# Row dots on VectorE in the first chain, turned blocks copied by ScalarE in the second: a decode backward pass on one core

## The chip, the cores and the metric

The kernel runs on one core of a Trainium2 chip. The metric is device time in microseconds (us) of one execution; lower is better. A core has TensorE (PE; its weight loads are listed as PEld), VectorE (DVE), ScalarE (ACT), GpSimd (POOL), SyncE (SP) and 16 DMA engines. Here SyncE issues the loads and GpSimd the stores.

## The reference

A transformer block for one decoded token in a batch of two, forward and backward: adaptive layer norm, attention over a cache of 8192 keys in 32 heads, then a gated MLP. The gradients of both caches are outputs, and they and the caches are nearly all of the traffic. The part that the change touches is the backward pass of the MLP, for each batch element b:

```python
h   = layernorm(x) * (1 + cb) + sb            # called h2 in the kernel, 512 wide
gate, up = h @ w1, h @ w3                     # w1, w3: 512 x 1376
out = (silu(gate) * up) @ w2                  # w2: 1376 x 512
# wanted here:  d_h2 = w3 @ d_up + w1 @ d_gate   (w1, w3 lie in SBUF with their 512 rows on partitions)
```

## The kernel before

The program is laid out in numbered slots; in each slot every engine gets a little work of several jobs. A head is a job of 8 slots. There are 64 heads (32 for each batch element), and each has two jobs: a *first pass* reads K and V (4 MiB); a *second pass* reads V again and writes the gradients of K and V (6 MiB). Between them stand two *chains*, one for each batch element, of small dependent steps: attention output, layer norm, MLP forward and backward. Second passes of an element can start only after its chain. So the order is: first passes alone; the first chain beside first passes; a mixed stage of first and second passes; the second chain beside second passes; second passes alone with the weight gradients; and a tail.

In both chains the gradient of h2 was made by turning: TensorE transposes eight 128x128 blocks of w3 or w1 (four in the last group of each) into PSUM, VectorE copies them to SBUF, TensorE multiplies them by the vector in the next slot. Twelve such groups take 13 slots.

```python
def turned_steps(put, groups, done):
    def tr(k):
        ...                                                     # cut
        for j, src in enumerate(blocks):
            nc.tensor.transpose(tp[:r, j, :], src, identb[:])
        kt = ktp.tile([P, GRP, P], BF16, name="kt", tag="kt")
        nc.vector.tensor_copy(kt[:r, 0:len(blocks), :], tp[:r, 0:len(blocks), :])
        st[("t", k)] = kt
    ...                                                         # cut
    for k in range(len(groups) + 1):
        put(1, lambda k=k: step(k))                             # one slot each
```

The length of the first chain decides how many first passes come before the second passes:

```python
E0 = CS0 + length(ch[0])
TC = E0 + 5
while len(sA) < NHD and s < TC:      # sA: first slots of first passes, sC: of second passes
    sA.append(s); s += NG            # NG = 8 slots
...                                  # then first and second passes in turn
CS1 = end_a(sA[NHD - 1]) + 1         # the second chain follows the last first pass
```

After each chain, `steps_do` turns blocks of the output projection in the same manner, one group of two heads at a time.

## Time and profile before

The median is 1759.24 us over 20 runs (1756.26 to 1765.01). The profile was taken in a run of 1762.17 us. From its page, the span, the busy times and the transfers:

```profile
span 1760.4 us, 55279 instructions
...
PE 1389.0 (79%) x24266; PEld 1243.7 (71%) x24266; DVE 1181.6 (67%) x1697; ACT 953.3 (54%) x1370; POOL 391.9 (22%) x685
...
DMA packets 114847, 713.59 MB, mean 405 GB/s; under 512 B 11392, under 2 KB 20300, under 8 KB 33196
```

| Stretch (us) | what runs | GB/s | DMA share |
|---|---|---|---|
| 40 to 280 | first passes alone | 416 | 1.01 |
| 360 to 500 | first chain and its wake | 388 | 1.00 |
| 500 to 1080 | mixed | 413 | 1.01 |
| 1080 to 1200 | second chain | 381 | 0.99 |
| 1250 to 1680 | second passes, weight gradients | 415 | 1.01 |
| 1690 to 1740 | tail | 393 | 0.97 |

No engine is busy all the time, but the DMA engines nearly are: the kernel is bound by its 713.59 MB. An engine's busy time matters only where it keeps transfers from being issued. There are two such places in the middle. The table by stretch (window; busy us and number of instructions of PE, PEld, DVE, ACT, POOL; granted TensorE clock, 1.00 being full speed; DMA share; GB/s) shows the first one, the first chain's turns and their wake (the shortage of transfers that follows them). DMA share is the mean busy share of the 16 DMA engines, which the view can give as slightly over 1:

```profile
core 0: us, PE busy (x) PEld busy (x) DVE busy (x) ACT busy (x) POOL busy (x), PEclk, DMA share, GB/s
420.00:440.00 20.00, 18.19 (x379) 16.21 (x378) 14.54 (x36) 8.50 (x12) 1.89 (x7) 1.00 1.00 401
440.00:460.00 20.00, 18.95 (x397) 18.01 (x393) 16.35 (x23) 13.41 (x21) 7.22 (x12) 1.00 0.98 373
460.00:480.00 20.00, 18.42 (x382) 16.27 (x383) 12.61 (x16) 13.35 (x19) 4.51 (x11) 1.00 1.00 387
480.00:500.00 20.00, 17.37 (x319) 16.32 (x317) 15.23 (x23) 9.47 (x13) 5.50 (x9) 0.91 1.00 390
```

and the second one, the second chain's turns:

```profile
1130.00:1140.00 10.00, 7.94 (x158) 7.69 (x156) 7.51 (x23) 6.64 (x11) 0.93 (x2) 0.50 0.91 357
1140.00:1150.00 10.00, 8.44 (x163) 8.14 (x161) 9.46 (x25) 4.05 (x4) 1.59 (x3) 0.67 0.91 343
1150.00:1160.00 10.00, 8.18 (x158) 7.68 (x155) 9.57 (x19) 3.57 (x6) 1.06 (x2) 0.83 0.99 350
1160.00:1170.00 10.00, 8.73 (x142) 8.47 (x139) 8.73 (x18) 3.27 (x4) 1.07 (x2) 0.66 0.91 333
```

In the first TensorE is busiest (18.2 of 20 us), in the second VectorE (up to 9.57 of 10). The timeline of VectorE (start, duration, line, operation) shows the pace of the first chain's turns. L689 is the copy of a turned group, one per slot; L885 copies the result of the group before:

```profile
408.32 0.69 DVE L689 COPY kt<-tp 128x1024 bf16<-128x1024 bf16 x1 [1.05 <-PE tp L687]
408.93 0.16 DVE L885 COPY dacc<-s_ps 128x4 f32<-128x4 f32 x1
...
410.52 0.69 DVE L689 COPY kt<-tp 128x1024 bf16<-128x1024 bf16 x1 [0.71 <-PE tp L687]
...
413.13 0.68 DVE L689 COPY kt<-tp 128x1024 bf16<-128x1024 bf16 x1
```

These copies start 2.2 to 2.6 us apart here; over the whole stretch a slot takes 2.15 us (the first and the last of the twelve results, in another group of the timeline, at 408.9 and 432.5 us). A slot of first passes alone takes 1.25 us: a head of 8 slots starts every 10.05 us. So the first chain makes compute fall behind.

### The profile page before, as it was taken

The numbers are of one execution on the slowest core, as the hardware profiler recorded it, in microseconds if no ns is written. First come the engines' busy times: TensorE is split into PE (matmuls) and PEld (weight loads), VectorE is DVE, ScalarE is ACT, GpSimd is POOL, SyncE is SP. The second block draws the span as 40 slices with busy tenths as digits, with TensorE's granted clock in tenths as the row PEclk, the third lists the DMA queues.
The fourth block names the chain that finished last, engine by engine and source line by source line (L and its number), as shares of the span: only waits on it lengthen the run. The fifth ranks groups of instructions, "written<-read, shape, count | busy, mean of one in ns | idle before, by whom it ended". The sixth has DMA issues, their size and how long they took to land. (4 is left out here: it accounts for less than half of the span.)

```text
span 1760.4 us, 55279 instructions
## 1 busy us (share of the span) xinstructions
PE 1389.0 (79%) x24266; PEld 1243.7 (71%) x24266; DVE 1181.6 (67%) x1697; ACT 953.3 (54%) x1370; POOL 391.9 (22%) x685
## 2 busy tenths in 40 slices
PE   6999999989877778777777877887678677866862
PEld 5999998878876767667677767787655555664662
DVE  2666666856767667666766766899666665765596
ACT  4666666653654554545455454534565566674752
POOL 0333333310222122212212222211112121211121
PEclk9999999988997887898788778668655555585685
DMA  9999999999999999999999999999999999999997
GB/s 381 418 418 416 418 417 389 418 377 410 384 409 423 415 422 414 409 412 406 413 415 413 405 411 400 380 365 424 423 413 419 409 405 419 403 422 424 417 381 298
DMA packets 114847, 713.59 MB, mean 405 GB/s; under 512 B 11392, under 2 KB 20300, under 8 KB 33196
## 3 DMA queue, kind: packets, MB, share of 16 engines
q1 hardware_dynamic: 73376, 425.81, 60.1%
q0 software_dynamic: 41216, 284.22, 38.9%
q8 instruction: 190, 3.11, 0.7%
q14 instruction: 53, 0.43, 0.1%
q10 hardware_dynamic: 12, 0.01, 0.0%
HBM read 425.79 MB, written 284.20 MB: 403 GB/s over the span
## 5 line engine op out<-in xcount | busy, mean ns | idle before, releaser
L371 ACT COPY kt<-tp 128x1024 bf16<-128x1024 bf16 x768 | 775.2, 1015 | 588.6 <-PE tp L366 572.8
L366 PE MATMUL tp<-identb,half 128*128 128x128 bf16 x8192 | 775.9, 251 | 4.8 <-DVE kt L369 2.0
L366 PEld LDWEIGHTS <-half 128*128 128x128 bf16 x8192 | 603.5, 113 | 120.0 <-issue 115.0
L1043 POOL DMA_DIRECT2D out_dram<-half x256 | 136.3, 532 | 987.4 <-DVE half L1038 805.5
L427 PE MATMUL m_ps<-ek,half 128*128 128x129 bf16 x4096 | 327.5, 222 | 0.0
L369 DVE COPY kt<-tp 128x1024 bf16<-128x1024 bf16 x256 | 176.0, 688 | 175.5 <-PE tp L366 173.7
L1015 PE MATMUL s_ps<-DO_bf,kt 128*128 128x1 bf16 x4096 | 191.9, 168 | 96.5 <-DVE kt L369 64.4
L1015 PEld LDWEIGHTS <-kt 128*128 128x128 bf16 x4096 | 188.8, 108 | 111.4 <-DVE kt L369 72.2
L386 PE MATMUL s_ps<-qT_bf,kt 128*128 128x1 bf16 x4096 | 177.7, 164 | 107.0 <-DVE kt L369 101.0
L427 PEld LDWEIGHTS <-half 128*128 128x128 bf16 x4096 | 248.0, 98 | 0.0
L386 PEld LDWEIGHTS <-kt 128*128 128x128 bf16 x4096 | 160.0, 98 | 113.0 <-DVE kt L369 105.1
L1163 ACT CAST stg<-m_ps 128x512 bf16<-128x512 f32 (+2 forms) x123 | 72.1, 592 | 114.4 <-DMA out_dram<-stg 90.3
L1162 PE MATMUL m_ps<-half 2*128 2x512 bf16 (+2 forms) x123 | 72.4, 589 | 28.8 <-ACT stg L1163 27.4
L449 PE MATMUL k_ps<-half,pz 128*32 128x512 bf16 x1024 | 67.2, 383 | 20.7 <-POOL pz L435 20.7
L449 PEld LDWEIGHTS <-pz 128*32 128x32 bf16 x1024 | 21.5, 96 | 41.0 <-POOL pz L435 23.0
L1263 ACT COPY kt<-tp 128x1024 bf16<-128x1024 bf16 x28 | 28.6, 1047 | 8.6 <-PE tp L1256 8.6
L398 DVE TENSOR_REDUCE nm<-s_ps 128x1 f32<-128x128 f32 x64 | 18.5, 289 | 20.3 <-PE s_ps L395 20.3
L395 PE MATMUL s_ps<-nident,rm 128*128 128x128 bf16 x64 | 15.4, 241 | 20.3 <-DVE rm L390 20.3
L1140 ACT CAST half<-m_ps 2x512 bf16<-2x512 f32 (+1 forms) x36 | 20.0, 564 | 21.0 <-DVE ds_26107 L1059 8.8
L1256 PE MATMUL tp<-identb,half 128*128 128x128 bf16 x224 | 20.7, 248 | 9.7 <-DMA half<-in_A_wq_dram 5.4
L711 PE MATMUL tp<-identb,half 128*128 128x128 bf16 x256 | 27.1, 271 | 0.0
L714 DVE COPY kt<-tp 128x1024 bf16<-128x1024 bf16 x32 | 22.0, 687 | 4.2 <-PE tp L711 4.2
(870 smaller groups left out, 1786.8 us busy)
## 6 DMA issues: line engine op xcount, KB each, us to landing
out_dram<-half POOLq DMA_DIRECT2D x256, 1024.0 KB, 12.9
half<-in_A_v_cache_dram SPq DMA_DIRECT2D x252, 1024.0 KB, 12.2
half<-in_A_k_cache_dram SPq DMA_DIRECT2D x128, 1024.0 KB, 19.6
out_dram<-stg POOLq DMA_DIRECT2D x22, 512.0 KB, 17.1
half<-in_A_wq_dram SPq DMA_DIRECT2D x8, 1024.0 KB, 16.7
half<-in_w_mod_dram SPq DMA_DIRECT2D x6, 1024.0 KB, 16.3
half<-in_B_w_dram SPq DMA_DIRECT2D x6, 1024.0 KB, 15.2
half<-in_A_wo_dram SPq DMA_DIRECT2D x4, 1024.0 KB, 20.5
```

Source lines behind the costliest of these rows:

```text
L366: nc.tensor.transpose(tp[:, j, :], block(j), identb[:])
L369: nc.vector.tensor_copy(kt[:], tp[:])
L371: nc.scalar.copy(kt[:], tp[:])
L386: nc.tensor.matmul(S_ps[i][:, cc:cc + 1], kt[:, j, :], qT_bf[:, h, b:b + 1], start=True, stop=True)
L427: nc.tensor.matmul(m[:, 0:P + 1], vb_(i, kk), t[:, kk % QK, 0:P + 1], start=(kk == 0), stop=(kk == KK - 1), skip_group_check=True)
L449: nc.tensor.matmul(kp["ps"][NR * j:NR * (j + 1), :], pz[:, o:o + NR], K[(i, kk // HK)][:, kk % HK:kk % HK + QP, :], start=False, stop=(h = ...
L711: nc.tensor.transpose(tp[:, n * NC + dc, :], wo_of(h, dc), identb[:])
L1015: nc.tensor.matmul(DP[n][:, cc:cc + 1], kt[:, j, :], DO_bf[:, b, h:h + 1], start=True, stop=True)
L1043: sq_.dma_start(src_of(dst, n)[:, hf * HK:(hf + 1) * HK, :], t[:])
L1162: nc.tensor.matmul(ps[:lw, 0:rw], rsl(ln, lc, lw), rsl(rn, rc, rw), start=True, stop=True)
L1163: nc.scalar.copy(st["t"][:lw, o:o + rw], ps[:lw, 0:rw])
L1263: nc.scalar.copy(kt[:], tp[:])
```

## The change

Intent: in the first chain, do w @ vector without turning. The vector is spread over all partitions as a row (TensorE and ScalarE, six steps), and VectorE multiplies it with the rows of w and sums along the free dimension in one instruction. In the second chain VectorE is already full, so there the turning stays and only the copy moves to ScalarE.

```diff
-            nc.vector.tensor_copy(kt[:r, 0:len(blocks), :], tp[:r, 0:len(blocks), :])   # turned_steps, now b=1 only
+            nc.scalar.copy(kt[:r, 0:len(blocks), :], tp[:r, 0:len(blocks), :])
@@ steps_do
-            nc.vector.tensor_copy(kt[:], tp[:])
+            if b == 0:
+                nc.vector.tensor_copy(kt[:], tp[:])
+            else:
+                nc.scalar.copy(kt[:], tp[:])
@@ steps_chain
+        if b == 0:
+            dot_steps(put)
+        else:
+            turn_steps(put)
+    def dot_steps(put):
+        def rows(v, vec, c0):
+            ...                                                  # cut: spread 4 chunks over partitions into PSUM
+            nc.scalar.copy(wn["w2f"][:, v * ROWV + c0 * P:v * ROWV + c0 * P + w], ps[:, 0:w])
+        def one(v, nm, kc, hi):
+            ...                                                  # cut
+            nc.vector.scalar_tensor_tensor(junk[:, 0:n], w, 1.0, wn["w2f"][:, o:o + n], ALU.mult, ALU.mult,
+                                           accum_out=dacc[:, kc, 2 * v + hi:2 * v + hi + 1])
+        ...                                                      # cut: 6 x put(1, rows)
+                put(2, lambda v=v, nm=nm, kc=kc: one(v, nm, kc, 0))     # 1024 columns
+                put(1, lambda v=v, nm=nm, kc=kc: one(v, nm, kc, 1))     # 352 columns
```

The dots take 30 slots in place of 13. By the layout code above, 40 first passes then come before the second passes in place of 38, and the second chain starts at slot 720 in place of 728. I call this the *new order* of heads, against the *old order*.

More of the change, by code (lines that the diff above doesn't have):

```diff
@@ L548, in load_w2 @@
     def load_w2():
-        wn["w2"] = hflat()[:].rearrange("p (k d) -> p k d", d=D)
+        wn["w2f"] = hflat()[:]
+        wn["w2"] = wn["w2f"].rearrange("p (k d) -> p k d", d=D)
         free["half"] -= 1
@@ L869, in steps_chain, with turn_steps @@
         put(1, p6)
+        if b == 0:
+            dot_steps(put)
+        else:
+            turn_steps(put)
+        return end_steps(put, out, b, hold)
+    ROWV = 3 * 512
+    def dot_steps(put):
+        def rows(v, vec, c0):
+            n = min(4, FC - c0)
+            ps = tps.tile([P, 4 * P], F32, name="rows", tag="tp")
+            w = 0
+            for k in range(n):
+                r = fsz(c0 + k)
+                nc.tensor.matmul(ps[:, k * P:k * P + r], vec[:r, c0 + k, 0:1].to_broadcast((r, P)),
+                                 identb[:r, :r], start=True, stop=True)
+                w = k * P + r
+            nc.scalar.copy(wn["w2f"][:, v * ROWV + c0 * P:v * ROWV + c0 * P + w], ps[:, 0:w])
+        def one(v, nm, kc, hi):
+            w = wn[(nm, hi)][:, kc, :]
+            n = w.shape[-1]
+            o = v * ROWV + hi * PW
+            junk = ktp.tile([P, GRP * P], BF16, name="junkb", tag="kt")
+            nc.vector.scalar_tensor_tensor(junk[:, 0:n], w, 1.0, wn["w2f"][:, o:o + n], ALU.mult, ALU.mult,
+                                           accum_out=dacc[:, kc, 2 * v + hi:2 * v + hi + 1])
+        pairs = list(enumerate((("w3", d_up_bf), ("w1", d_gate_bf))))
+        for v, (nm, vec) in pairs:
+            for c0 in range(0, FC, 4):
+                put(1, lambda v=v, vec=vec, c0=c0: rows(v, vec, c0))
+        for v, (nm, vec) in pairs:
+            for kc in range(NC):
+                put(2, lambda v=v, nm=nm, kc=kc: one(v, nm, kc, 0))
+                put(1, lambda v=v, nm=nm, kc=kc: one(v, nm, kc, 1))
+    def turn_steps(put):
+        b = B - 1
         groups = []
@@ L889, in steps_chain, with end_steps, sums @@
                            for nm, fcs, mm in groups], dacc_done)
+    def end_steps(put, out, b, hold):
+        nd = 4 if b == 0 else dacc.shape[-1]
+        def sums():
+            hold["ps"] = scr(2 * NC)
+            nc.tensor.matmul(hold["ps"], onesf[:], hold["both"][:].rearrange("p t k -> p (t k)"),
+                             start=True, stop=True)
         def q1():
-            nc.vector.tensor_reduce(d_h2[:, :, b], dacc[:], AX.X, ALU.add)
+            nc.vector.tensor_reduce(d_h2[:, :, b], dacc[:, :, 0:nd], AX.X, ALU.add)
             both = tmp.tile([P, 2, NC], F32, name="both2", tag="both2", bufs=2)
```

## The prediction

> **What bounds the kernel.** The transfers. The page's bandwidth row gives 713.59 MB at a mean of 405 GB/s; the table by stage shows a DMA share of 1.01 at 416 GB/s (40 to 280 us, first passes only), at 413 (500 to 1080, mixed) and at 415 (1250 to 1680, last passes). Waits of the load queue end with an earlier load or a store (760 us), rarely with compute. The Trainium skill ("DMA: Bandwidth & Descriptors", "Measured") has 425 GB/s for a 16 MB stream; the best 40 us here show 425. So engine work gains time only where DMA runs dry.
>
> It does so in few places (windows of 10 us): 420 to 450 (383 to 354 GB/s, share down to 0.95) and 450 to 500 (about 389), which are the first chain and its wake; 1130 to 1190 (333 to 363, share down to 0.91), the second chain; and the tail from 1680 (385, share 0.95, VectorE 62.1 of 65 us busy), which the change leaves alone.
>
> **First chain (b=0).** Removed: 12 groups of 8 transposes, a VectorE copy (0.69 us), thin matmuls and a 0.15 us copy: 10 us of VectorE, about 10 us of TensorE (192 instructions at some 50 ns). The timeline shows those slots at 2.2 us each (405 to 432 us); a slot of first passes alone takes 1.25 us. So compute falls behind, buffers fill, and DMA runs short at 440 us. Added: 6 ScalarE copies of 512 columns (about 0.6 us) and 16 row dots. The existing 512-column dot takes 0.69 us plus a 0.14 us accumulator read that mostly overlaps; at one element per cycle my estimate is 1.22 us for 1024 columns, 0.53 for 352: 15 us of VectorE. Per three slots: 2.4 us for first passes (154.8 of 240 us busy) plus 1.85, so 1.4 us a slot against 1.25 of DMA. The chain grows by 17 slots (13 become 30); two more heads run before second passes start. The total number of slots does not change, so a longer chain by itself costs nothing; it holds four weight buffers longer, which leaves 11 of 21, enough. Expected: 2 to 4 us gained.
>
> **Second chain (b=1).** It starts 8 slots earlier, at the same length. In 1137 to 1172 us VectorE is busy 31.9 of 35 us, ScalarE 12.7; a slot takes 2.2 us against 1.89 for DMA (6.3 MB a head at 415 GB/s). Moving the copies takes 0.69 us a slot off VectorE and adds 1.01 us to ScalarE, whose slot becomes about 1.9 us: near the DMA pace, but now ScalarE and TensorE (30.4 of 35 us busy, granted clock 0.70) bind. Expected: 2 to 4 us. The 16 later copies of output-projection blocks run where DMA is already full: nothing.
>
> **Sum.** About 6 us gained, less new stalls: 1753.5 us; range 1743 to 1761. Chances: faster by over 2% 0.02, within 2% 0.96, slower 0.02.
>
> **What would show it.** DMA share 0.99 or more and over 400 GB/s in the wake of the first chain; VectorE under 75% and ScalarE over 80% in the second chain's turns, GB/s up from 342 to about 380; dots of 1.2 and 0.5 us, 1.4 us a slot; the tail unchanged with VectorE full.
>
> **What would make it wrong.** Wide dots longer than 1.3 us; the longer hold of weight buffers starving loads; shared copy buffers making transposes wait for dots; ScalarE, in order, stalling the second chain more than VectorE did; slack refilled elsewhere, so nothing is gained.

## The result, and the profile after

The changed kernel takes 1751.20 us in the median of 10 runs (1749.16 to 1752.70). The ratio is 0.9951, with a 95% interval of 0.9942 to 0.9960: 8 us, half a per cent, and so within the 2% to which the prediction gave a chance of 0.96. (Ratios here are the mean time of one kernel's fast runs over that of the other's of the same rounds, so not quite the ratio of the medians quoted.) The page of its profile:

```profile
span 1752.4 us, 54974 instructions
...
PE 1374.2 (78%) x24112; PEld 1230.7 (70%) x24112; DVE 1170.5 (67%) x1677; ACT 980.1 (56%) x1404; POOL 393.8 (22%) x685
...
DMA packets 114845, 713.56 MB, mean 407 GB/s; under 512 B 11392, under 2 KB 20300, under 8 KB 33196
```

The first chain's wake, in the same windows as above:

```profile
420.00:440.00 20.00, 19.89 (x406) 18.10 (x404) 19.77 (x37) 12.83 (x18) 7.26 (x12) 1.00 1.00 412
440.00:460.00 20.00, 19.09 (x393) 17.69 (x393) 16.98 (x38) 12.42 (x20) 6.41 (x11) 1.00 1.01 418
460.00:480.00 20.00, 18.87 (x386) 17.63 (x379) 13.39 (x18) 11.52 (x18) 5.81 (x9) 1.00 1.01 420
480.00:500.00 20.00, 14.90 (x276) 13.69 (x274) 17.16 (x25) 9.69 (x13) 5.57 (x10) 0.83 1.01 423
```

From 440 to 500 us the transfers now run at 418 to 423 GB/s, where they ran at 373 to 390. VectorE is nearly full from 420 to 440 (19.77 of 20 us), and the transfers still run at 412 GB/s there (401 before). The tile that the dots write shows their lengths (ns, minimum/median/maximum):

```profile
L898 DVE SCALAR_TENSOR_TENSOR junkb<-half x16: 507/878/1251, 413.9 to 444.7; 128x1024 bf16<-128x1024 bf16 x8, 128x352 bf16<-128x352 bf16 x8
L898 DVE DVE_READ_ACCUMULATOR junkb<-half x16: 75/76/85, 415.1 to 445.2; 128x1 f32 x16
```

The 1024-column dots take 1.22 us and the 352-column ones 0.52. The 24 slots of dots take from 413.9 to 445.3 us, 1.31 us each.

The second chain, which now comes earlier:

```profile
1110.00:1120.00 10.00, 7.80 (x164) 7.57 (x163) 7.54 (x21) 5.74 (x11) 1.06 (x2) 0.50 0.89 359
1120.00:1130.00 10.00, 8.29 (x166) 8.02 (x166) 7.26 (x20) 6.20 (x7) 1.06 (x2) 0.71 0.93 306
1130.00:1140.00 10.00, 8.59 (x197) 7.98 (x195) 8.60 (x15) 9.99 (x14) 1.36 (x3) 1.00 1.00 369
1140.00:1150.00 10.00, 6.88 (x149) 6.16 (x147) 9.29 (x20) 7.08 (x11) 1.83 (x4) 0.98 1.00 406
```

ScalarE is full for a while (9.99 of 10 us). The dip is shorter but not shallower. The copies of the results of the second chain's twelve turned groups show the pace (first and last start), in the kernel before and in the changed one:

```profile
L885 DVE COPY dacc<-s_ps x12: 149/155/157, 1146.8 to 1171.0; 128x4 f32<-128x4 f32 x12
```

```profile
L927 DVE COPY dacc<-s_ps x12: 156/162/167, 1126.4 to 1145.2; 128x4 f32<-128x4 f32 x12
```

Eleven slots took 24.2 us and now take 18.8.

To see where time comes from in a kernel that is bound by transfers, I added up the bytes moved: the GB/s of each 20 us window times 20 us, over a stretch. At 415 GB/s, 1 MB is 2.4 us. The figures of all profiles are in one table further down. Against the kernel before, the changed kernel is 2.4 MB ahead between 360 and 500 us (56.70 against 54.32 MB) and 1.2 MB between 1080 and 1200 (46.94 against 45.74). That looks like a simple sum of two local gains. The experiments ask whether it is one.

### The profile page after: what moved, and what is told of

Same layout as the page of the kernel before. It is cut to its first block, busy times and chain, and to the rows that moved or that the text cites. A ratio compares the mean times of both kernels' runs of the same rounds, so it can differ in the third digit from the quotient of the medians.

```text
span 1752.4 us, 54974 instructions
## 1 busy us (share of the span) xinstructions
PE 1374.2 (78%) x24112; PEld 1230.7 (70%) x24112; DVE 1170.5 (67%) x1677; ACT 980.1 (56%) x1404; POOL 393.8 (22%) x685
## 5 line engine op out<-in xcount | busy, mean ns | idle before, releaser
L371 ACT COPY kt<-tp 128x1024 bf16<-128x1024 bf16 x768 | 775.0, 1016 | 534.3 <-PE tp L366 526.2
L369 DVE COPY kt<-tp 128x1024 bf16<-128x1024 bf16 x256 | 176.0, 688 | 187.3 <-PE tp L366 183.2
L1313 ACT COPY kt<-tp 128x1024 bf16<-128x1024 bf16 x28 | 28.6, 1048 | 8.3 <-PE tp L1306 8.2
L1306 PE MATMUL tp<-identb,half 128*128 128x128 bf16 x224 | 20.7, 247 | 9.8 <-DMA half<-in_A_wq_dram 5.5
L718 ACT COPY kt<-tp 128x1024 bf16<-128x1024 bf16 x16 | 16.2, 1012 | 14.4 <-PE tp L712 13.8
```

Source lines behind the costliest of these rows:

```text
L369: nc.vector.tensor_copy(kt[:], tp[:])
L371: nc.scalar.copy(kt[:], tp[:])
L1313: nc.scalar.copy(kt[:], tp[:])
```

## The experiments

Theory A was that each half of the change gives its own local gain and the two add up. Rivals: it is enough to thin the old work out over more slots (B), or the new order of heads is the gain (C). All ratios are against the kernel before on the same chip in the same rounds; all kernels gave correct results.

### Dots alone (e1)

The changed kernel, with both copies back on VectorE for b=1.

```diff
-            nc.scalar.copy(kt[:r, 0:len(blocks), :], tp[:r, 0:len(blocks), :])
+            nc.vector.tensor_copy(kt[:r, 0:len(blocks), :], tp[:r, 0:len(blocks), :])
```
(and the same in `steps_do`)

> The first chain's row dots alone; the second chain's copies stay on VectorE. Theory A (the gain is the sum of two local ones: less TensorE work in the first chain, less VectorE work in the second): about 5 us under the kernel before (1754), with the wake of the first chain at 415 to 420 GB/s as in the changed kernel, and the second chain's turns still 2.2 to 2.3 us a slot. Rival (the whole gain is from one place, the first chain): the full 8 us, 1751.

Measured: 1756.19 us, ratio 0.9980 (0.9966 to 0.9994), runs from 1751.79 to 1760.52. The wake is gone, as in the changed kernel (56.86 MB from 360 to 500 us). The whole gain is not from here; but 3.5 us are less than the 2.5 MB would be worth (6 us at 415 GB/s). The run with idle slots (e5) shows one reason: it has about 1 MB of that lead from the new order alone, and gains no time.

### Copies alone (e2), and again (e2b)

The kernel before with ScalarE copies where b=1, in `turned_steps` and `steps_do`.

```diff
+            if b == 0:
                 nc.vector.tensor_copy(kt[:r, 0:len(blocks), :], tp[:r, 0:len(blocks), :])
+            else:
+                nc.scalar.copy(kt[:r, 0:len(blocks), :], tp[:r, 0:len(blocks), :])
```

> The second chain's copies on ScalarE alone; the first chain still turns. Theory A: about 3 us under the kernel before (1756), turn slots of the second chain at 1.8 us in place of 2.3, the dip at 440 to 500 us unchanged (373 to 390 GB/s). Rival that the copies move costs as much on ScalarE as it saves: 1759, no gain.

> The copies alone, timed again for the same reason. By the bytes moved in its own trace, 0.8 MB more than before in the second chain's window (1080 to 1200 us), about 2 us: 1757. If the second look gives 1759 again, the 2 us gained there are given back later.

Measured: 1759.02 us, ratio 1.0001 (0.9989 to 1.0013), and 1759.07 us, 0.9999 (0.9987 to 1.0012). The turns did speed up (11 slots in 20.1 and 19.8 us), but the time did not move. This is a miss of theory A: the halves, 0.9980 and 1.0000, don't make 0.9951.

### Turns spread over 30 slots (e4)

```diff
-            put(1, lambda k=k: step(k))
+            n = 1 if b == 1 else 3 if k % 3 == 0 and k < 12 else 2
+            put(n, lambda k=k: step(k))
```

> The kernel before, with the first chain's 12 turns spread over 30 slots, as many as the row dots take; same schedule of heads as the changed kernel. Theory A (TensorE work taken out): the same TensorE work is only thinned, slots of about 1.7 us for 24 slots, compute lags as far behind; gain 0 to 2 us (1757 to 1759). Rival B (pacing: it is enough not to crowd the work into 13 slots): the gain of the dots alone, about 5 us (1754).

Measured: 1758.52 us, ratio 0.9990 (0.9977 to 1.0003). The mean is 1.8 us lower, and the interval holds 1. The 5 us that rival B asked for lie outside the interval. Against the 3.5 us that the dots alone gave (0.9966 to 0.9994) the two intervals overlap, so the time alone doesn't tell the two apart; the trace does: 55.06 MB from 360 to 500 us against 56.86, and the first product of the second passes (see e12) at 466.7 us against 458.5. Thinning leaves most of the lag.

### Turns, then 17 idle slots (e5)

```diff
         for k in range(len(groups) + 1):
             put(1, lambda k=k: step(k))
+        if b == 0:
+            put(17, lambda: None)
```

> The kernel before, with 17 empty slots after the first chain's turns, so the order of heads is that of the changed kernel (40 first passes before the second passes, second chain 8 slots earlier) with the old work. Theory A: no gain from the order itself, 1758 to 1760, perhaps 1 us from two more light heads in which the first chain's lag is made up. Rival C (the gain is the order of heads, not the work): about 5 us (1754).

Measured: 1760.70 us, ratio 1.0000 (0.9988 to 1.0012). The new order by itself is worth nothing that can be told from noise (2 us either way), as the prediction had it. Rival C falls in its simple form.

### The changed kernel again (a2)

No edit.

> The changed kernel unaltered, timed again beside the others of this call, because the two halves alone (ratios 0.998 and 1.0001) did not add up to 0.9951. If the halves add and the first timing was lucky: 1754 to 1756. If the two halves help each other: 1750 to 1752 again.

Measured: 1750.03 us, ratio 0.9954 (0.9942 to 0.9966). The result is repeated; the halves do help each other.

### Idle slots and copies (e12)

The edits of e5 and e2 together: new order, ScalarE copies, no dots.

```diff
+            if b == 0:
                 nc.vector.tensor_copy(kt[:r, 0:len(blocks), :], tp[:r, 0:len(blocks), :])
+            else:
+                nc.scalar.copy(kt[:r, 0:len(blocks), :], tp[:r, 0:len(blocks), :])
...
+        if b == 0:
+            put(17, lambda: None)
```

> No dots: the first chain turns as before and then idles 17 slots, and the second chain's copies are on ScalarE, so the order of heads and the second chain are those of the changed kernel and only the first chain's arithmetic differs. Theory A: about 3 us over the changed kernel (1754 to 1755), because by 500 us its trace moved 1.2 MB less. Rival C (order of heads plus ScalarE copies is the whole gain, the dots are only a way to make the chain long): equal to the changed kernel, 1751.

Measured: 1753.99 us, ratio 0.9970 (0.9958 to 0.9982), all five runs between 1753.66 and 1754.32. Two things follow. At the same order and with the same copies, the dots are worth 3 us (1754.0 against 1751.1 in the mean of the changed kernel's runs). The intervals of the two ratios still overlap; the pair with VectorE copies (e5 against e1) has 3.5 us, the same way. And copies and new order, each worth nothing alone, are together worth 5 us.

The first multiplication of the second passes shows what the dots do. It is the same step of the schedule in both kernels. First the kernel with idle slots and copies, then the changed one:

```profile
467.98 1.22 DVE L1046 TENSOR_TENSOR half<-DOr,e 128x2048 bf16<-128x2048 bf16 x1
```

```profile
459.16 1.22 DVE L1088 TENSOR_TENSOR half<-DOr,e_11343 128x2048 bf16<-128x2048 bf16 x1
```

It comes 8.8 us earlier with the dots: that is the lag of compute that the turns caused and that idle slots do not cure. Part of the wake is still there too; from 460 to 480 us the kernel with idle slots and copies has 385 GB/s, where the changed one has 420:

```profile
460.00:480.00 20.00, 18.87 (x395) 17.78 (x396) 17.02 (x26) 12.71 (x21) 7.66 (x12) 1.00 0.98 385
```

### Dots crowded into the old 13 slots (e13)

```diff
-                put(1, lambda v=v, vec=vec, c0=c0: rows(v, vec, c0))
+                put(1 if (3 * v + c0 // 4) % 2 else 0, lambda v=v, vec=vec, c0=c0: rows(v, vec, c0))
-                put(2, lambda v=v, nm=nm, kc=kc: one(v, nm, kc, 0))
-                put(1, lambda v=v, nm=nm, kc=kc: one(v, nm, kc, 1))
+                put(1, lambda v=v, nm=nm, kc=kc: one(v, nm, kc, 0))
+                put(1 if kc == 3 else 0, lambda v=v, nm=nm, kc=kc: one(v, nm, kc, 1))
```

> The changed kernel with the first chain's dots crowded into the 13 slots that the turns took, so the order of heads is that of the kernel before; dots and ScalarE copies are kept. Without the copies the order was worth nothing (17 idle slots: 1.0000), with them 5 us (1.0001 against 0.997). Reading 1 (the order of heads decides what the copies are worth): dots add 3 to 4 us to copies alone and no more, 1755 to 1756. Reading 2 (the copies need a first chain without its wake, by whatever means): 1751 as the changed kernel. By 500 us I expect 2 MB or more over the kernel before, since VectorE needs 1.95 us a slot where TensorE needed 2.2.

Measured: 1756.52 us, ratio 0.9986 (0.9974 to 0.9999). The time is nearer to reading 1 (which asked for 1755 to 1756) than to reading 2 (1751): at the old order dots and copies together give 2.5 us. But the bytes missed: 55.06 MB from 360 to 500 us, half a MB over the kernel before and not 2. The crowded dots fill VectorE, and transfers run short again:

```profile
410.00:430.00 20.00, 14.97 (x276) 13.81 (x274) 20.00 (x43) 9.23 (x14) 7.77 (x10) 0.91 0.99 392
```

So this run does not separate the order from the lag, and reading 2, which asks for a first chain without its wake, was not put to the test: crowding kept most of the lag (the first second-pass product at 445.5 us, against 448.4 and 447.2 in two profiles of the kernel before).

### The first chain's copies on ScalarE (e6)

The kernel before, edited in `turned_steps` only, with the cases of e2 exchanged.

```diff
+            if b == 1:
                 nc.vector.tensor_copy(kt[:r, 0:len(blocks), :], tp[:r, 0:len(blocks), :])
+            else:
+                nc.scalar.copy(kt[:r, 0:len(blocks), :], tp[:r, 0:len(blocks), :])
```

> The kernel before with the first chain's turn copies on ScalarE (the second chain's stay on VectorE): 8 us of work off VectorE, none off TensorE. If TensorE binds those slots (9.8 of 10 us busy at 400 to 410 us): slots stay at 2.2 us, 54.3 MB between 360 and 500 us as before, 1758 to 1760. If VectorE binds them: slots under 2 us and most of the dots' gain, 1755 to 1756.

Measured: 1758.07 us, ratio 0.9995 (0.9982 to 1.0007). The time agrees with "TensorE binds", the trace does not: eleven slots took 20.7 us (405.5 to 426.2) where they took 23.6, and 55.66 MB were moved from 360 to 500 us. So VectorE was part of what held those slots. Before, then this kernel, over the turns:

```profile
405.00:432.00 27.00, 24.05 (x487) 21.24 (x486) 17.95 (x37) 10.16 (x14) 2.50 (x9) 0.98 1.00 404
```

```profile
405.00:427.00 22.00, 21.45 (x470) 20.39 (x468) 11.17 (x26) 18.55 (x26) 2.06 (x10) 1.00 1.01 418
```

The list of waits says where. TensorE's waits for VectorE from 400 to 435 us in the kernel before, then in this kernel (total us, times, longest):

```profile
PE s_ps L386 <- DVE dacc L885: 2.9, 9, 0.6
```

```profile
PE s_ps L386 <- DVE dacc L888: 0.3, 1, 0.3
```

TensorE waited for the small copy to `dacc`, which comes behind the copy of the turned group in VectorE's order (408.32 and 408.93 us in the timeline). 2.6 us of that wait went, and the eleven slots are 2.9 us shorter.

Some 5 to 6 us of the lag went (the same product at 442.2 us), and no time was gained. A byte lead early is not a gain for sure.

### Dots in both chains (e7)

```diff
-        if b == 0:
-            dot_steps(put)
-        else:
-            turn_steps(put)
+        dot_steps(put, b)
```
(with column b of the vectors in `rows`)

> The row dots in the second chain too, in place of turns with ScalarE copies; that chain then has 30 slots for them and fewer second passes are left to the mixed stage. VectorE is the fullest engine beside the second chain (31.9 of 35 us in the kernel before), and second passes take it about 1.4 us of a 1.9 us slot; three slots with 1.8 us of dots make 2.0 us a slot over 24 slots. Theory A: slower than the changed kernel by 2 to 4 us (1753 to 1755), a long dip to about 390 GB/s. Rival (dots are simply the better form): 1749 or less.

Measured: 1753.27 us, ratio 0.9966 (0.9952 to 0.9981), runs from 1749.63 to 1756.66. The median came as theory A had it, but not for its reason: there is no long dip to 390. VectorE is full, and the transfers run at 404:

```profile
1110.00:1160.00 50.00, 30.11 (x465) 28.00 (x461) 49.97 (x80) 23.13 (x35) 6.93 (x13) 0.71 1.01 404
```

The stretch from 1080 to 1200 us moved 48.70 MB, the most of all kernels. But this profile is of its fastest run, 1749.63 us, as fast as the changed kernel; the runs spread over 7 us, and the interval overlaps that of the changed kernel (0.9942 to 0.9966 in a2). So neither "slower" nor "faster" than the changed kernel is shown, and why the runs spread stays open.

### The tail's copies on ScalarE too (e9)

```diff
+        dve = g in (2, 6) and sC[n] < max(sC) - 8 * NG
-        kts[("c", n, g)] = transposes(lambda j: vb_(("c", n), g * GRP + j), g in (2, 6))
+        kts[("c", n, g)] = transposes(lambda j: vb_(("c", n), g * GRP + j), dve)
```

> The changed kernel with the last 8 heads' two VectorE copies of turned V blocks moved to ScalarE too. In the tail VectorE is busy 9.97 of 10 us at 391 GB/s; a head takes it 11.6 us, and 1.4 us less would be at the 10.2 us that stores need at 410 GB/s. If VectorE binds the tail: 3 to 4 us under the changed kernel (1747 to 1748), 405 GB/s or more from 1680 on. If the stores themselves bind: no change, 1751, VectorE at about 88%.

Measured: 1753.96 us, ratio 0.9969 (0.9957 to 0.9980): not faster than the changed kernel. The tail itself behaved as expected of VectorE binding it; changed kernel, then this one:

```profile
1670.00:1730.00 60.00, 38.33 (x699) 36.14 (x696) 59.80 (x63) 33.91 (x47) 12.22 (x23) 0.77 0.97 393
```

```profile
1670.00:1730.00 60.00, 40.37 (x769) 33.54 (x765) 59.76 (x58) 46.53 (x63) 13.82 (x26) 0.86 1.01 409
```

The rate rose from 393 to 409 GB/s. The run that was profiled was its slowest (1757.14 us), and that profile ran at 413 GB/s from 1200 to 1600 us where the changed kernel's has 416, 1.5 MB less by the sum of 20 us windows, though the edit changes nothing there (its last VectorE copy of a V block is at 1609 us). This was meant as a better version; neither it nor any other variant has a median under that of the changed kernel.

### A second profile of the kernel before (b2)

No edit.

> The kernel before, for a second profile, to know how far the bytes moved in each stretch differ between two profiles of one kernel: the first profile was taken in a run of 1762 us, 3 us over the median. Expected: within 0.3 MB up to 500 us and in the second chain's window (1080 to 1200 us), within 0.8 MB in the long stages.

Measured: 1760.29 us, one run. This profile has 46.54 MB from 1080 to 1200 us, where the first had 45.74. The expectation of 0.3 MB missed (so did, barely, the stretch from 360 to 500 us, with 0.4 MB), and with it goes the reading that the copies gain 0.8 MB at the old order: e2 has 46.56 MB there, just what the second profile of the kernel before has.

### The table

Bytes moved in each stretch (MB, one profile each), the start of the first second-pass product, and the ratio:

| Kernel | order | copies, b=1 | 360 to 500 | 500 to 1080 | 1080 to 1200 | 1200 to 1640 | product at (us) | ratio |
|---|---|---|---|---|---|---|---|---|
| before | old | VectorE | 54.32 | 239.74 | 45.74 | 182.94 | 448.4 | 1 |
| before again (b2) | old | VectorE | 54.68 | 240.10 | 46.54 | 182.18 | 447.2 | 1 |
| e6, first chain's copies on ScalarE | old | VectorE | 55.66 | 239.90 | 45.92 | 182.74 | 442.2 | 0.9995 |
| e2 copies | old | ScalarE | 54.52 | 240.56 | 46.56 | 182.56 | 447.2 | 1.0001 |
| e2b copies | old | ScalarE | 54.16 | 240.14 | 46.64 | 183.18 | 448.1 | 0.9999 |
| e13 dots crowded | old | ScalarE | 55.06 | 240.26 | 46.62 | 181.96 | 445.5 | 0.9986 |
| e4 turns spread | new | VectorE | 55.06 | 239.60 | 46.28 | 182.02 | 466.7 | 0.9990 |
| e5 turns, idle | new | VectorE | 55.50 | 239.16 | 46.06 | 182.80 | 467.1 | 1.0000 |
| e1 dots | new | VectorE | 56.86 | 239.98 | 46.10 | 182.54 | 458.5 | 0.9980 |
| e12 turns, idle | new | ScalarE | 55.38 | 239.44 | 46.98 | 183.52 | 468.0 | 0.9970 |
| changed | new | ScalarE | 56.70 | 239.44 | 46.94 | 183.20 | 459.2 | 0.9951 |
| changed again (a2) | new | ScalarE | 56.92 | 240.00 | 47.64 | 183.30 | 458.5 | 0.9954 |
| e9, tail | new | ScalarE | 56.72 | 239.50 | 47.26 | 181.58 | 459.4 | 0.9969 |
| e7, dots in both | new, fewer second passes mixed (23 for 25) | none | 56.70 | 239.68 | 48.70 | 182.28 | 459.2 | 0.9966 |

The columns differ in how far they can be trusted. From 360 to 500 us the four profiles that turn in 13 slots with VectorE copies, without idle slots, lie between 54.16 and 54.68 and the five with dots in 30 slots between 56.70 and 56.92: that is shown. From 1080 to 1200 us at the new order, the three with VectorE copies have 46.06 to 46.28 and the four with ScalarE copies 46.94 to 47.64: shown too, 1.1 MB between the means. That stretch in dots alone, then in the changed kernel:

```profile
1080.00:1200.00 120.00, 96.52 (x1707) 92.22 (x1706) 103.95 (x221) 50.00 (x71) 16.35 (x31) 0.70 0.99 384
```

```profile
1080.00:1200.00 120.00, 98.95 (x1713) 93.87 (x1712) 92.58 (x198) 72.08 (x98) 17.90 (x33) 0.68 0.99 391
```

At the old order the means differ by 0.5 MB (46.07 and 46.61) and the ranges all but touch (up to 46.54, from 46.56). From 1200 to 1640 us the figures spread by 1.9 MB, and 1.5 MB of that is between two profiles of the same code (the changed kernel and e9, up to 1600 us); so no difference in it is told as a cause. A profile is also of one run: the two of the kernel before are of runs 2.9 and 1.1 us above its median, that of the changed kernel is 3.0 us above and that of e7 3.6 us below. So a single difference can be off by 3 us, some 1.2 MB.

## Why the prediction was right or wrong

The time, 1753.5 us predicted and 1751.2 measured, was right, and so was the bound, as far as the gain can be placed: the two stretches in which the traces show more bytes are those where transfers ran below their rate.

- **First chain, "2 to 4 us gained".** The mechanism was right: compute fell behind in the turns, and without them the wake is gone (418 to 423 GB/s from 440 to 500 us, share 1.01). In bytes, 2.3 MB lie between the means of the profiles before (54.50) and after (56.81), 5.6 us at 415 GB/s. In time, the dots against idle slots at the same order are worth 3 us with ScalarE copies (e12 against a2) and 3.5 us with VectorE copies (ratios 1.0000 and 0.9980), within the forecast. At the same order the bytes agree with this: 1.43 MB (56.81 against 55.38) and 1.36 MB (56.86 against 55.50), 3.4 and 3.3 us. The other 0.9 to 1.0 MB of the lead is there with the idle slots too, without dots, and gained no time in e5; what becomes of it is not settled, since the later columns are no surer than that.
- **The sizes of the pieces.** Dots of 1.22 and 0.52 us were forecast as 1.22 and 0.53; slots of dots of 1.31 us as 1.4. The Trainium skill ("VectorE: DVE Perf Modes", "The TRN2 errata — SBUF-src ops pay a fixed extra latency per instruction") gives PSUM-to-SBUF copies on ScalarE as 172 cycles plus the elements over a speed-up factor, at 1.2 GHz; with no speed-up that is an estimate of 997 ns for 1024 columns. ScalarE's copies of that shape took 1012 ns in the trace before, and the moved ones 1031 ns in the mean, so the cost of moving the copies was well known beforehand.
- **"10 us of VectorE, about 10 us of TensorE" as what the dots free.** The prediction counts both and does not say which of them set the 2.2 us of a slot. With the TensorE work untouched and only the copies on ScalarE (e6) the slots fell from 2.15 to 1.88 us: VectorE's copies, through the wait shown above, cost 0.27 us a slot. That leaves 1.88 us against the 1.25 of a slot without the chain, with TensorE 21.45 of 22 us busy; with the dots a slot takes 1.31.
- **"A longer chain by itself costs nothing".** Right as said (e5, 1.0000). What it left out is that the copies are worth something only together with the new order.
- **Second chain, "2 to 4 us" from the copies.** As an independent term it failed: at the old order the copies gave nothing, in two trials. At the new order they give 5 us (e5 1.0000 to e12 0.9970; e1 0.9980 to a2 0.9954), more than forecast. The sum came out well because the change has both, and that was luck: the prediction names the earlier start of the second chain but gives no reason why the copies should need it. The traces show about 1.1 MB, 2.6 us, of it in the second chain's stretch. Where the rest comes from, and why the order matters, stays open.
- **The signs named.** VectorE under 75% in the second chain's turns was wrong: from 1123 to 1146 us it is busy 19.33 of 23 us (84%). Its work fell from 2.0 to 1.4 us a slot, but the slots also got shorter, from 2.20 to 1.71 us; ScalarE at 90% (20.66 of 23) was right. The rate did not rise to 380 GB/s within the turns (354 in that window); the gain is a shorter dip. The tail is nearly as it was, as forecast (from 1690 to 1740 us 393 GB/s before and 397 after; VectorE 49.83 of 50 us busy there before, and 59.80 of 60 from 1670 to 1730 us after).
- **"The 16 later copies of output-projection blocks: nothing".** Not tested apart from the others.

## What to carry to other kernels

In a kernel that is bound by transfers, look for the stretches where compute falls behind, and measure how far: the time at which one fixed step of the schedule runs (459.2 against 468.0 us here) says it better than busy shares. It is a sign and not yet a gain: in e6 that step came 5 to 6 us earlier and the kernel was no faster. Time the halves of a change apart and together, because a gain can need both (here 1.0000, 1.0000 and 0.9970 for two edits and their sum). And take a second profile of the same kernel before a difference of one MB or two microseconds is given a cause.

## What the Trainium skill lacked or had wrong

- "VectorE: DVE Perf Modes", the perf-mode tier table: it has no row for a multiply with a sum along the row (`scalar_tensor_tensor` with an accumulator). In bf16 from SBUF it took 1222 ns for 1024 columns and 516 ns for 352, which is 1.05 ns a column, about one per cycle at the 0.96 GHz that the page gives, with about 146 ns fixed; the accumulator read adds 76 ns, most of it overlapped.
- "DMA: Bandwidth & Descriptors", "Where 436 GB/s comes from": it says without a condition that for transfers between HBM and SBUF the HBM side binds, at about 358 GB/s. This program on one core read at 416 GB/s for 240 us and moved 405 GB/s in the mean of the whole span. The sentence needs the condition that the same page gives under "Measured", where 358 GB/s is the share of a core with both cores of the pair streaming.
- No page gives a size for how far the rate can fall while the DMA engines count as busy ("Perfetto Trace Analysis", "Identifying the Most-Contended Engine", only warns that occupancy misleads for DMA): here a share of 1.00 went with 387 and 390 GB/s in the wake of the turns and with 1.01 at 420 and 423 without them. What lowers the rate at a full share was not found.
